# Clustered attention and a gated FFN on one core: another load order and other steps for the preparation of the heads

## The chip, the cores and the metric

The kernel runs on one core of a Trainium2 chip. The metric is device time in microseconds (us), the median of several executions. A profile of one further execution gives the times of single instructions; they are counted from the start of its span. The engines are TensorE (PE, with its weight loads PEld), VectorE (DVE), ScalarE (ACT), GpSimd (POOL) and SyncE (SP, which here only issues transfers). Every engine works through its own list of instructions in the order in which the program wrote them.

## The reference, cut to what matters

```python
batch, n_heads, seq, head_dim = (4, 8, 768, 64);  n_clusters = 16
q_assign = argmax(einsum('bhsd,hcd->bhsc', q_n, c_n), -1)      # k_assign alike
mask = q_assign[..., :, None] == k_assign[..., None, :]
scores = where(mask, matmul(q, k.T) / sqrt(D), -1e9)
attn = softmax(scores);  a = matmul(attn, v)
x = a.transpose(0, 2, 1, 3).reshape(3072, 512)
out = (sigmoid(x @ w_gate) * (x @ w_val)) @ w_out              # 512 -> 1536 -> 512
```

Each query and each key of a head goes to the nearest of 16 centroids, and a query attends only to the keys of its own cluster. The result of all eight heads is the input of a gated feed-forward network.

## The kernel before, in words

**Tiling.** A batch has 8 heads in 4 pairs, 768 positions in 6 chunks of 128. For each head the kernel builds one tile `T` (128 rows, 12 chunks: 6 of keys, 6 of queries). Rows 0 to 63 hold the high half of the fp32 values in fp16; rows 64 to 127 first hold the low half, which the cluster logits need, and then rows 64 to 79 are overwritten with a one-hot row of the cluster: 1 for a key, and -1920 at the wrong clusters for a query. One matmul of a key chunk with the queries then gives score and mask together.

**Steps.** The program is a list of 384 steps, 96 for each batch, which one loop at the end writes out. A step is one scores matmul (`do_scores`, L615: 128 keys by 384 queries, PE L622) and its exponential on ACT (L627). Three steps later in the first batch, and two later in the others, follow the three matmuls with the values (`do_av`, L630, PE L640). In the first batch all heads run first with the first half of the queries (steps 0 to 47, six for each head: head 0 at 0, head 1 at 6, head 4 at 24), then with the second half (48 to 95). From step 57 on, matmuls of the feed-forward network (gate L447, value L467, output L487) are woven in between.

**Preparation of a head.** In the first batch, `first` (L821) makes a head's tile in pieces: `hi` (cast to fp16, L834) and `lo` (the remainder, L841), each once for keys (0) and queries (1); `tu` (six or three 128x128 transposes on PE, L862); `ev` (copy out of PSUM, L873 on ACT, L875 on DVE); `lg` (logits with the centroids, PE L365); `pk` (row maximum L890 and comparison L898, DVE); `ot` (transposes of the one-hot rows, PE L922); and `pl` (copies of these 16 rows into `T`, L943 and L947 on DVE, L945 on ACT). `h2lo1` is piece `lo` of the queries of head 2. `r0` to `r3` are the second halves of the queries of a pair (`rest`, L949). The pieces of the first head are written out by hand (L1057 to L1085 and `lead_in`, L1107). The later batches (`pair_prep`, L1195) use `sp` (split), `tn` (turn of the whole tile by a transposing DMA, L354), `lg`, `pk`, `ot` (one-hot turn by a transposing DMA, L1220) and `hp` (row copies by DMA, `hop`, L428); `b2p0tn0` is the turn of the first head of pair 0 in batch 2. `vc` casts the values (POOL, L282), `vs` sums them (PE L313 in the first batch). `turn_x` (L658) transposes a pair's result for the network.

**What sets the order.** `SCHED`, a table by hand, gives each piece a step. `at` (L672) files the piece under that step, and `run_bg` (L678) writes out all pieces that are due, lowest number first, and pieces of equal number in the order in which they were filed. A number below the current step less a half is raised to it: at the start that is -4.5, so all numbers below -4.5 mean the first slot ahead of step -3. Entries with a final `E` choose the engine of a piece (`A` ACT, `D` DVE, `P` POOL). `nd` entries put small matmuls on constant data into the PE list ahead of a step (`dummies`, L693, does so in the lead-in; `dm` entries give the counts), and `ns` entries say how much of the network is written at each step. A piece whose input is late holds its engine, and all that stands behind it on that engine.

**Loads.** The loop at L1038 issues the first batch's loads on SP: first those of head 0, then `v0, k1, q1, v1, k2, q2, v2, k3, q3, v3` (`k2` is the keys of pair 2, 384 KB; a `q` here is the first half of the queries, 192 KB). The second halves of the queries (`ql`) and the loads of later batches are pieces with steps of their own.

**PSUM.** Scores, logits and value sums share four buffers (`ring`, L147); transposes, one-hot turns and the network's output share two (`op`, L149).

Of the kernel before, what the change touches and what calls it, by code (L numbers as in the profile page):

```python
# [10 lines left out]
AF = mybir.ActivationFunctionType  # L11
ALU = mybir.AluOpType
# [76 lines left out]
def kernel(  # L89
# [164 lines left out]
    def centroid_b():  # L254
        DVE.tensor_scalar(r0, r0, 1e-6, None, ALU.add)
        DVE.reciprocal(r0, r0)
        ACT.activation(c2, cen.unsqueeze(1).to_broadcast([128, 2, D]), AF.Copy, scale=r0)
# [26 lines left out]
    def v_sum(b, p):  # L284
        r, st = RAW["v", b, p], {}

        def one():
            st["a"] = vsp.tile([128, 2, 3, 64], FP, tag="va3", name="va3")
            DVE.tensor_tensor(st["a"], r[:, :, 0:3], r[:, :, 3:6], ALU.add)

        def two():
            a = st["a"]
            s = st["s"] = vss[(b * NP + p) % len(vss)]
            t = vsp.tile([128, 2, 64], FP, tag="va1", name="va1")
            DVE.tensor_tensor(t, a[:, :, 0], a[:, :, 1], ALU.add)
            DVE.tensor_tensor(s[:, :, 0:64], t, a[:, :, 2], ALU.add)
# [375 lines left out]
    def at(i, f):  # L672
        bg.setdefault(max(i, step_no[0] - 0.5), []).append(f)

    def plan(name, step, f):
        at(SCHED.get(name, step), f)
# [518 lines left out]
    def pair_prep(b, p, use):  # L1195
# [26 lines left out]
        def hops(e):  # L1222
            for s in range(2):
                hop(st["ot"], 2 * e + s, T[b, 2 * p + e], 6 * s, 6)
# [105 lines left out]
```

## Time and profile before

| | |
|---|---|
| time, median of 3 runs | 328.78 us (328.36 to 329.84) |
| profiled execution, own time | 330.25 us |
| its span, first to last instruction | 328.4 us |
| PE busy | 321.7 us, 98% |
| ACT busy | 239.5 us, 73% |
| DVE busy | 187.5 us, 57% |
| POOL busy | 107.9 us, 33% |
| read from and written to memory | 28.34 MB and 6.29 MB |

The profiled execution lies 1.47 us above the median, and 1.85 us of it lie outside the span. A row of the timeline has start, length, engine, line, operation, what it writes and reads, shape, count, and in brackets how long the engine stood idle before it and whom it waited for. Matmuls are pipelined: the length of one includes its way through the array, so a row of one matmul of 384 columns shows about 0.33 us although the next can start about 0.16 us after it, and an engine shown as busy may still be held up for a short time. Starts are exact, ends of matmuls are modelled.

### The profile page before, as it was taken

How to read it: one execution, taken by the hardware profiler on the slowest of the kernel's cores; microseconds unless marked ns; L12 is line 12 of the kernel's file. 1: busy time of each engine (PE TensorE's matmuls, PEld its weight loads, DVE VectorE, ACT ScalarE, POOL GpSimd, SP SyncE). 2: the span in 40 equal slices, each digit the busy share in tenths (PEclk: the TensorE clock that was granted, in tenths of full speed). 3: DMA queues.
4: the chain of work that ended last, by engine and by line, in shares of the span. 5: the costliest groups of instructions: out<-in, count | busy, mean ns of one | idle time of the engine just before them, and what ended most of it. 6: DMA issues, size and time to landing. Idle time of an engine off the chain costs nothing.

```text
span 328.4 us, 8945 instructions
## 1 busy us (share of the span) xinstructions
PE 321.7 (98%) x3405; PEld 209.2 (64%) x3405; DVE 187.5 (57%) x531; ACT 239.5 (73%) x547; POOL 107.9 (33%) x149
## 2 busy tenths in 40 slices
PE   8899999999999999999999999999999999999996
PEld 4688866766666666666566655666566665654654
DVE  6688747778658567556556654666534322441431
ACT  6497998887989898877778777788778877332421
POOL 5866464334434375424133343413301111000000
PEclk9799999999999999999999999999999999999999
DMA  6999987728986996975775473752631012102002
GB/s 199 360 247 165 241 164 127 183 62 209 237 173 185 170 213 145 267 151 131 184 216 107 144 134 90 210 121 50 140 92 36 2 26 76 46 1 85 12 0 96
DMA packets 77994, 45.14 MB, mean 137 GB/s; under 512 B 56896, under 2 KB 75008, under 8 KB 77952
## 3 DMA queue, kind: packets, MB, share of 16 engines
q1 hardware_dynamic: 73984, 39.73, 48.6%
q0 software_dynamic: 3680, 4.72, 8.8%
q8 instruction: 26, 0.43, 0.5%
q10 hardware_dynamic: 288, 0.13, 0.1%
q14 instruction: 16, 0.13, 0.1%
HBM read 28.34 MB, written 6.29 MB: 105 GB/s over the span
## 4 chain that ended last, share of the span: by engine, by line
PE 91%; DMA 4%; SPq 2%; ACT 1%; POOL 1%; issue 0%; DVE 0%
PE v L467 18%; PE o L487 18%; PE g L447 18%; PE sc L622 18%; PE av L640 10%; DMA T<-hl 2%; PE lg L378 2%; DMA kraw<-in_k_dram 2%; PE lg L365 1%; PE t_ps L862 1%; ACT es L627 1%; PE o_end L519 1%; PE oh_ps L922 1%; SPq L185 1%; PE sc L619 1%; SPq L429 1%
## 5 line engine op out<-in xcount | busy, mean ns | idle before, releaser
L627 ACT ACTIVATE es<-sc 128x384 f16<-128x384 f32 x384 | 176.2, 494 | 39.2 <-PE sc L622 34.5
L622 PE MATMUL sc<-T 128*128 128x384 f16 x384 | 119.2, 327 | 0.3 <-DVE T L947 0.2
L640 PEld LDWEIGHTS <-es 128*128 128x128 f16 x1152 | 81.8, 98 | 49.3 <-issue 0.2
L640 PE MATMUL av<-va,es 128*128 128x65 f16 x1152 | 97.7, 194 | 0.0
L474 DVE SCALAR_TENSOR_TENSOR hT<-th,v 128x384 f16<-128x384 f32 x96 | 53.1, 553 | 65.7 <-PE av L640 42.5
L467 PE MATMUL v<-xTb,wv 128*128 128x384 f16 x384 | 78.1, 326 | 0.0
L447 PE MATMUL g<-xTb,wg 128*128 128x384 f16 x384 | 78.0, 326 | 0.0
L487 PE MATMUL o<-wo,hT 128*128 128x512 f16 x276 | 75.1, 379 | 0.0
L334 POOL TENSOR_TENSOR xp<-t,rec 128x192 f16<-128x192 f32 (+1 forms) x46 | 29.5, 642 | 129.0 <-DVE rec L331 78.6
L455 ACT ACTIVATE th<-g 128x384 f32<-128x384 f32 x96 | 47.2, 491 | 25.3 <-DVE hT L474 17.9
L447 PEld LDWEIGHTS <-wg 128*128 128x128 f16 x384 | 37.2, 97 | 20.4
L467 PEld LDWEIGHTS <-wv 128*128 128x128 f16 x384 | 37.4, 98 | 20.1 <-issue 0.2
L622 PEld LDWEIGHTS <-T 128*128 128x128 f16 x384 | 37.2, 97 | 0.7 <-DVE T L947 0.4
L487 PEld LDWEIGHTS <-hT 128*128 128x128 f16 x276 | 26.7, 97 | 16.2
L329 DVE TENSOR_TENSOR t<-av,sv 128x195 f32<-128x195 f32 (+1 forms) x46 | 20.1, 437 | 23.8 <-PE av L640 20.6
L1203 POOL TENSOR_TENSOR hl<-kraw,hl 128x384 f16<-128x384 f32 x22 | 20.7, 943 | 25.2 <-DVE hl L1202 13.2
L1203 POOL TENSOR_TENSOR hl<-qraw,hl 128x384 f16<-128x384 f32 x22 | 21.6, 982 | 11.9 <-DVE hl L1202 11.9
L390 DVE TENSOR_TENSOR lgs<-lg,lglo 128x192 f32<-128x192 f32 (+1 forms) x25 | 8.7, 348 | 16.4 <-ACT lglo L384 15.9
L496 ACT ACTIVATE ob<-o 128x512 f32<-128x512 f32 x15 | 8.9, 596 | 10.8 <-PE o L487 10.7
L282 POOL CAST va<-vraw 128x768 f16<-128x768 f32 x16 | 13.4, 840 | 2.1 <-DMA vraw<-in_v_dram 2.1
L494 DVE TENSOR_SCALAR ob<-o 128x512 f32<-128x512 f32 x8 | 5.5, 691 | 13.4 <-PE o L487 13.3
L378 PE MATMUL lg<-cm,T 128*128 128x32 f16 x288 | 11.1, 177 | 0.2 <-DMA T<-hl 0.2
(117 smaller groups left out, 245.3 us busy)
## 6 DMA issues: line engine op xcount, KB each, us to landing
vraw<-in_v_dram SPq DMA_DIRECT2D x16, 384.0 KB, 5.1
out_dram<-ob SPq DMA_DIRECT2D x23, 256.0 KB, 2.3
kraw<-in_k_dram SPq DMA_DIRECT2D x15, 384.0 KB, 4.3
qraw<-in_q_dram SPq DMA_DIRECT2D x12, 384.0 KB, 4.2
wg<-in_moe_w_gate_dram POOLq DMA_DIRECT2D x2, 768.0 KB, 8.6
wv<-in_moe_w_val_dram POOLq DMA_DIRECT2D x2, 768.0 KB, 7.6
wo<-in_moe_w_out_dram POOLq DMA_DIRECT2D x2, 768.0 KB, 8.6
qraw<-in_q_dram SPq DMA_DIRECT2D x7, 192.0 KB, 6.7
```

The costliest lines, as they stand in the source:

```text
L329: DVE.tensor_tensor(t[:, 0:nq, :], av, sv, ALU.add)
L334: (eng or POOL).tensor_tensor(x, t[:, 0:nq, 0:64], bcast(rec[:, 0:nq], 64), ALU.mult)
L378: PE.matmul(out=lg[:, bass.ts(i, 32)], lhsT=t[:, c, :], rhs=cm[:, h].rearrange("p s n -> p (s n)"), start=True, stop=True,)
L447: PE.matmul(out=g[:, 0:n], lhsT=wg[fc // WQ][:, dc, fc % WQ, :], rhs=xT[:, dc, t0 : t0 + n], start=(dc == 0), stop=(dc == NDC - 1),)
L455: ACT.activation(th[:, 0:n], g[:, 0:n], AF.Tanh, scale=0.5)
L467: PE.matmul(out=w[:, 0:n], lhsT=wv[fc // WQ][:, dc, fc % WQ, :], rhs=xT[:, dc, t0 : t0 + n], start=(dc == 0), stop=(dc == NDC - 1),)
L474: DVE.scalar_tensor_tensor(hT[:, fc, 0:n], st[1][:, 0:n], 1.0, w[:, 0:n], ALU.add, ALU.mult)
L487: PE.matmul(out=o, lhsT=hT[:, fc, bass.ts(t, 128)], rhs=wo[fc // WON][:, fc % WON, :], start=(fc == 0), stop=(fc == NFC - 1),)
L622: PE.matmul(out=sc.rearrange("p (c t) -> p c t", t=128), lhsT=s["k"], rhs=s["q"], start=True, stop=True,)
L627: ACT.activation(es, sc, AF.Exp, scale=SCALE)
L640: PE.matmul(out=av[:, s["c0"] + i, :], lhsT=s["es"][:, bass.ts(i, 128)], rhs=VA[b, p][:, e, s["j"], :], start=(first and i == 0), stop=(la ...
L1203: POOL.tensor_tensor(hl[:, :, 64:128], r, hl[:, :, 0:64], ALU.subtract)
```

## The change

241 entries of the table differ. Nearly all move a piece by half a step to four steps; these are the ones that the text below speaks of, one entry to a line:

```diff
+    "lo": ["k1", "v0", "q1", "y0", "v1", "k3", "q2", "q3", "k2", "v2", "v3"],
-    "h1lo1": -3.0, "h1tu1": -0.5, "h1ev0": -0.5, "h1ev1": 0,
+    "h1lo1": -37.5, "h1tu1": -38.5, "h1ev0": -3.5, "h1ev1": -3.5,
-    "h1lo1E": "D",
-    "h1pl0": 2.5, "h1pl1": 1.5,
+    "h1pl0": 1.5, "h1pl1": 3.5, "h1pl1E": "A",
-    "h2hi0": -4.0, "h2hi1": -0.5, "h2hi1E": "P", "h2lo0": -1.5, "h2lo1": 0,
+    "h2hi0": -8.5, "h2hi1": -8.5, "h2hi1E": "A", "h2lo0": -3.5, "h2lo1": -1.5,
-    "vc00": -4.0, "vs00": 1.5,
+    "vc00": -1.0, "vs00": 4.0,
-    "r0hi": 11.0,
+    "r0hi": 6.5,
-    "h3ev1E": "A", "h4pl1E": "A",
+    "h6ev0E": "A",
-    "h4hi0": 1.0, "h4lo0": 5.0, "h4tu0": 10.0, "h4lg": 16.5, "h4pk": 17.0, "h4ot": 20.0,
+    "h4hi0": 2.0, "h4lo0": 4.0, "h4tu0": 9.0, "h4lg": 15.0, "h4pk": 17.5, "h4ot": 21.0,
-    "dm1": 2, "dm4": 3,
+    "dm1": 1, "dm4": 4,
...
+    "b2p0tn0": -47, "b2p0lg0": -35.5, "b2p0lk": 3.5,
-    "b1p1hp0": -19.5, "b1p3ot": -23.5, "b1p3hp1": -12.5,
+    "b1p1hp0": -13.5, "b1p3ot": -19.0, "b1p3hp1": -14.0,
```

Ahead of the change `b2p0tn0` took the value -50 from `b2tn0`, `b2p0lg0` was -37.5, and `b2p0lk` took -0.5 from `b2lk`. `y0` in the new load order issues nothing. In the lists of instructions that the two programs give, PE has 45 in place of 40 of the small matmuls that the `nd` entries add, one of 128 columns less ahead of the first transposes (`dm1`), and one more behind the first scores (`dm4`). All other matmuls, and all transfers, are the same in kind and number; on ACT, DVE and POOL, casts and copies change their engine.

The code gains branches that the table does not switch on; they add no instruction:

```diff
+        cw = cen.unsqueeze(1).to_broadcast([128, 2, D])
+        if SCHED.get("c2d", 0):
+            DVE.tensor_scalar(c2, cw, r0, None, ALU.mult)
...
-    def v_sum(b, p):
+    def v_sum(b, p, eng=None):
...
         def hops(e):
+            if SCHED.get("hop2", 0):
...
-                at(use + o + d_, lambda b=b, p=p, side=side: load(SP, side, b, p))
+                at(use + o + d_, lambda b=b, p=p, side=side: load(
+                    (ACT if SCHED.get("lda", 0) else POOL) if side in SCHED.get("ldp", "") and NP * b + p >= SCHED.get("ldb", 5) else SP, side, b, p))
```

More of the change, by code (lines that the diff above doesn't have):

```diff
@@ L256, in centroid_b @@
         DVE.reciprocal(r0, r0)
-        ACT.activation(c2, cen.unsqueeze(1).to_broadcast([128, 2, D]), AF.Copy, scale=r0)
+        cw = cen.unsqueeze(1).to_broadcast([128, 2, D])
+        if SCHED.get("c2d", 0):
+            DVE.tensor_scalar(c2, cw, r0, None, ALU.mult)
+        else:
+            ACT.activation(c2, cw, AF.Copy, scale=r0)
     def centroid_c():
@@ L282, in v_cast @@
         (cast or POOL.tensor_copy)(va[:, h, :, 0:64], RAW["v", b, p][:, h])
-    def v_sum(b, p):
+    def v_sum(b, p, eng=None):
         r, st = RAW["v", b, p], {}
+        eng = eng or DVE
         def one():
             st["a"] = vsp.tile([128, 2, 3, 64], FP, tag="va3", name="va3")
-            DVE.tensor_tensor(st["a"], r[:, :, 0:3], r[:, :, 3:6], ALU.add)
+            eng.tensor_tensor(st["a"], r[:, :, 0:3], r[:, :, 3:6], ALU.add)
         def two():
@@ L294, in two @@
             t = vsp.tile([128, 2, 64], FP, tag="va1", name="va1")
-            DVE.tensor_tensor(t, a[:, :, 0], a[:, :, 1], ALU.add)
-            DVE.tensor_tensor(s[:, :, 0:64], t, a[:, :, 2], ALU.add)
+            eng.tensor_tensor(t, a[:, :, 0], a[:, :, 1], ALU.add)
+            eng.tensor_tensor(s[:, :, 0:64], t, a[:, :, 2], ALU.add)
         def rest():
@@ L1184 @@
             vf = {}
-            plan(f"vs0{p}", u - 3 if p else 4, lambda p=p, vf=vf: (vf.update(f=v_sum(0, p)), vf["f"][0]()))
-            at(SCHED.get(f"vs0{p}", u) + SCHED.get(f"vt0{p}", 1), lambda vf=vf: (vf["f"][1](), vf["f"][2]()))
+            plan(f"vs0{p}", u - 3 if p else 4, lambda p=p, vf=vf: (vf.update(f=v_sum(0, p, POOL if SCHED.get(f"vq{p}", 0) else DVE)), vf["f"][0]()))
+            at(SCHED.get(f"vs0{p}", u) + SCHED.get(f"vt0{p}", 3), lambda vf=vf: (vf["f"][1](), vf["f"][2]()))
         else:
@@ L1222, in hops @@
         def hops(e):
+            if SCHED.get("hop2", 0):
+                SP.dma_start(
+                    out=T[b, 2 * p + e][64:80].rearrange("x (s c) t -> s x c t", s=2),
+                    in_=st["ot"].rearrange("(y x) c t -> y x c t", x=32)[2 * e : 2 * e + 2, 0:16],
+                )
+                return
             for s in range(2):
```

139 rows, old and new, of the table SCHED are left out of this document.

## The prediction, made before the changed kernel ran

> **What bounds the kernel now.** I read the page's busy times and its chain of waits first, then the table of stretches of 8 us.
>
> ```profile
> PE 321.7 (98%) x3405; PEld 209.2 (64%) x3405; DVE 187.5 (57%) x531; ACT 239.5 (73%) x547; POOL 107.9 (33%) x149
> ...
> PE 91%; DMA 4%; SPq 2%; ACT 1%; POOL 1%; issue 0%; DVE 0%
> ```
>
> ```profile
> 0.00:8.00 8.00, 6.46 (x62) 4.07 (x62) 5.22 (x29) 4.93 (x11) 4.32 (x14) 1.00 0.66 195
> 8.00:16.00 8.00, 6.55 (x94) 5.20 (x92) 5.81 (x18) 3.32 (x8) 6.59 (x11) 0.79 1.08 362
> 16.00:24.00 8.00, 7.77 (x150) 6.58 (x147) 6.22 (x21) 7.92 (x20) 5.42 (x9) 1.00 1.12 255
> 24.00:32.00 8.00, 7.90 (x150) 6.95 (x150) 6.82 (x23) 6.75 (x16) 5.06 (x8) 1.00 0.97 162
> ...
> 104.00:112.00 8.00, 7.79 (x91) 5.14 (x90) 4.50 (x14) 7.30 (x19) 3.67 (x4) 1.00 1.26 237
> ```
>
> The columns of the second are the stretch, its length, busy time of PE, PEld, DVE, ACT and POOL, granted PE clock, DMA share and GB/s. PE carries 91% of the chain. It stands idle 1.54 us in the first 8 us and 1.45 in the next, then 0.23, 0.10, and in the stretch at 104 once more 0.21. Everything else is PE's own list of matmuls, which the change leaves as it is except for a few dummies. So the change can only gain in the first 30 us and at single waits later. In the second stretch PE also had a clock of 0.79, and from 16 to 24 us ACT is as full as PE (7.92 of 8).
>
> The timeline shows where PE loses time at the start:
>
> ```profile
> 7.24 0.34 PE L922 MATMUL oh_ps<-identh,oh 128*128 128x128 f16 x3
> ...
> 7.63 0.83 POOL L282 CAST va<-vraw 128x768 f16<-128x768 f32 x1 [2.11 <-DMA vraw<-in_v_dram]
> ...
> 8.41 0.34 PE L622 MATMUL sc<-T 128*128 128x384 f16 x1 [0.21 <-DVE T L947]
> ...
> 9.20 0.51 ACT L834 CAST hl<-kraw 128x384 f16<-128x384 f32 x1 [1.31 <-DMA kraw<-in_k_dram]
> ...
> 9.61 0.48 ACT L627 ACTIVATE es<-sc 128x384 f16<-128x384 f32 x1
> ...
> 10.00 0.47 ACT L873 COPY T<-t_ps 128x384 f16<-128x384 f16 x1
> ...
> 10.52 0.31 PE L365 MATMUL lg<-cm,T 128*128 128x16 f16 x6 [0.56 <-ACT T L873]
> ...
> 10.75 0.51 PE L862 MATMUL t_ps<-identh,hl 128*128 128x128 f16 x6
> ...
> 11.67 0.34 PE L862 MATMUL t_ps<-identh,hl 128*128 128x128 f16 x3 [0.40 <-POOL hl L841]
> ...
> 11.85 0.48 PE L622 MATMUL sc<-T 128*128 128x384 f16 x1
> ...
> 12.36 0.92 ACT L627 ACTIVATE es<-sc 128x384 f16<-128x384 f32 x2 [1.90 <-PE sc L622]
> ```
>
> The first scores start at 8.41, the second only at 11.85. Between them lies a chain: the keys of pair 1 (`k1`) land at 9.2, ACT stands with their cast at the head of its list, the copy of head 1's queries out of PSUM (`h1ev1`) comes at 10.00, PE's logits wait for it until 10.52, and the last transposes of head 2 wait for POOL until 11.67.
>
> **The change part by part: the start.** Its prices:
>
> ```profile
> 3.59 0.47 SPq L196 DMA_DIRECT2D qraw<-in_q_dram  x1
> ...
> 4.52 0.55 POOL L841 TENSOR_TENSOR hl<-qraw,hl 128x192 f16<-128x192 f32 x1 [0.89 <-ACT hl L834]
> ...
> 6.32 0.34 DVE L834 CAST hl<-qraw 128x192 f16<-128x192 f32 x1
> ...
> 10.64 0.34 POOL L834 CAST hl<-qraw 128x192 f16<-128x192 f32 x1
> ```
>
> ```profile
> DMA to landing us min/median/max: 2.9/6.2/7.3
> ```
>
> The last line is for the query loads of the first 17 us. `k1` takes the place of `v0` and should land at 7.6; `v0` lands at 9.2. `q1` stands behind both as before: 3.59 + 6.2 = 9.8, not ahead of the 9.2 of the load that it follows, and not after 10.64, where its cast began without a wait.
>
> *First scores.* The transposes of head 1's queries (`h1tu1`) now stand ahead of the six logits, five dummies and three one-hot turns at 7.24, and their low part (`h1lo1`) is on POOL. The cast ends at 6.32 + 0.34 = 6.66, the low part at 7.21, 7.27 with a hand-over of 0.06. Then three transposes (a step of 0.055 each, from six in 0.51 against three in 0.34), six logits (0.15) and five dummies (0.28) bring the turns from 7.24 to about 7.9. The first scores come 0.66 later, at 9.07. That alone costs nothing, since the second scores wait for the chain through ACT, which ends after them in either order.
>
> *Second scores.* ACT casts `k1` early, but the cast of `q1` moves from POOL to ACT, ahead of `h1ev1`. ACT waits until 9.8, casts (0.34) and copies (0.47): 10.6, against 10.00 + 0.47 = 10.47 before. PE's logits start 0.13 later, at 10.65, the six transposes at 10.88. The three that waited for POOL do not wait now: their low part starts when ACT's cast ends (10.14) and ends at 10.7. Six steps of 0.055 and the 0.18 from 11.67 to 11.85 give 11.39 in place of 11.85: **-0.45**. With `q1` at 9.2 it would be -1.05, at 10.64 +0.4; I take the median landing and keep both ends.
>
> [...]
>
> **The two loads that come later, or are wanted earlier.**
>
> ```profile
> 9.76 3.06 SPq L196 DMA_DIRECT2D qraw<-in_q_dram  x4
> ...
> 12.71 0.63 POOL L834 CAST hl<-kraw 128x384 f16<-128x384 f32 x1
> ...
> 14.06 0.94 POOL L229 DMA_DIRECT2D wg<-in_moe_w_gate_dram  x1
> ...
> 16.08 0.91 POOL L841 TENSOR_TENSOR hl<-kraw,hl 128x384 f16<-128x384 f32 x1
> ...
> 16.44 1.92 ACT L627 ACTIVATE es<-sc 128x384 f16<-128x384 f32 x4
> ...
> 18.28 0.50 PE L862 MATMUL t_ps<-identh,hl 128*128 128x128 f16 x6
> ```
>
> `k2` goes behind `k3`, `q2` and `q3`, 768 KB or 2.2 us at 362 GB/s. It had landed by 12.71, so it is there by 14.9. POOL then needs the cast (0.63), the issue of the gate weights (0.94), a query cast (0.34) and the low part (0.91): 17.7. Head 4's transposes started at 18.28; with PE 0.45 earlier they are wanted at 17.8. Cost nothing, and up to 0.4 if PE gains more than that. `r0hi` moves on ACT from step 11 to behind the eighth exponential. Its load, first of the four at 9.76, lands by 9.76 + 7.3 = 17.1; the eighth of the exponentials (third of the four at 16.44) ended at about 17.9, less 0.45 is 17.4. Again nothing, and up to 0.6 if ACT is much earlier. `v0` lands 1.6 later, and its cast stands three POOL operations later; the first matmuls with values wait for the first exponential too, now at 10.6.
>
> **Waits that go, and dummies.**
>
> ```profile
> 15.75 0.79 ACT L873 COPY T<-t_ps 128x768 f16<-128x768 f16 x1
> ...
> 23.48 0.26 PE L640 MATMUL av<-va,es 128*128 128x65 f16 x3
> ...
> 23.97 0.49 PE L922 MATMUL oh_ps<-identh,oh 128*128 128x128 f16 x6 [0.23 <-DVE T L875]
> ...
> 25.71 0.48 ACT L945 ACTIVATE T<-oh_ps 16x384 f16<-16x384 f16 x1
> ```
>
> ```profile
> 110.81 0.32 PE L622 MATMUL sc<-T 128*128 128x384 f16 x1
> ...
> 111.35 0.47 PE L378 MATMUL lg<-cm,T 128*128 128x32 f16 x12 [0.21 <-DMA T<-hl]
> ```
>
> The one-hot turns of head 4 could follow the value matmuls 0.09 after 23.48, but start 0.40 later, when DVE has emptied their PSUM buffer of head 5's transposes. The change puts head 4's logits 1.5 steps and that copy (`h5ev0`) 0.5 earlier, and the turns one step later: **-0.40**, at worst 0. The copy of head 4's query rows (0.48) leaves ACT for DVE, just ahead of head 4's scores: I take half, **-0.25**, between 0 and -0.48. In its place ACT gets a copy of 768 columns for head 6 (0.79), which the 1.25 us that ACT is idle from 24 to 32 should hide.
>
> At 111.35 the logits of batch 2's first head wait for its turn. The scores ahead take 0.16, so 0.38 is lost. The logits go two steps later and the turn three; if it lands when it did, behind loads that were issued ahead of it, the wait goes, and if it lands later with its issue, it grows by a step (0.6). I take **-0.20**, between -0.38 and +0.6. The other moves in later batches lie under a full PE: nothing to gain, and two new waits like this one, 0.8, is what I allow for. Five more dummies cost 5 x 0.055: **+0.28**; the one less (`dm1`) stands where PE waits.
>
> **Sum.** -0.45 - 0.40 - 0.25 - 0.20 + 0.28 = -1.02. Against the profiled execution's own 330.25 us (span 328.4 and 1.85 around it) that is 329.2. The median of the runs shown is 328.78, 1.47 less; I carry the same difference over: **327.8 us**.
>
> **The rivals.**
>
> *The clock stays up: 326.5 us.* The 0.79 from 8 to 16 us:
>
> ```profile
> 12.55 0.85 PE L922 MATMUL oh_ps<-identh,oh 128*128 128x128 f16 x6
> ...
> 16.22 0.50 PE L922 MATMUL oh_ps<-identh,oh 128*128 128x128 f16 x6
> ```
>
> Six turns take 0.85 behind the long gap and 0.50 later. At half clock, 0.21 x 8 / 0.5 = 3.4 us of the stretch, or 1.7 us of lost work; I price it at 1.4, since PE waits in part of it. If two scores ahead of 11.85 are work enough, that goes, less a little for `k2`: -1.3 on the forecast. For it: more matmuls in the gap; against it: the gap from 9.07 to 11.4 is still mostly waiting. [...]
>
> *What is gained is waited for again: 328.8 us.* POOL is busy 6.59 of 8 us and stands behind `k2`, ACT behind `q1` and `r0hi`. If these are later than I take them, PE's 0.45 is used up at head 4's transposes, and the two waits of 0.65 at heads 4 and 5 come back at heads 5 and 6; the dummies and batch 2 cancel.
>
> *ACT becomes the bound: 330.7 us, slower.* The first exponential moves from 9.61 to about 10.6 (+1.0), behind the cast of `q1`. ACT gains a cast (0.34), the row copy `h1pl1` (0.48) and the copy for head 6 (0.79), and loses copies of 0.47 and 0.48: +0.66. From 16 to 24 ACT is already full. If the exponentials set the pace to the end of the first batch's lead, this and the dummies add 1.9. It decides if ACT's waits of 1.90 ahead of 12.36 and after it do not shrink by 1.6 together; I think that they shrink by about that, since the second scores come earlier.
>
> **How the numbers follow.** Forecast 0.45 (its own range 327.1 to 328.5), clock 0.22, waited for again 0.21, ACT 0.12. Low end: the clock's case with the wider start, 326.0. High end 330.0, short of the ACT case: with it and the tails below 326.0, no more than 2 in 10 are left out. Half a per cent, about what a measurement of this kernel can tell from no change, is 1.64 us: below 327.14 is faster, above 330.42 slower. Faster: the clock's 0.22 and 0.08 of the forecast, 0.30. Slower: 0.12. Within: 0.58.
>
> **What the new profile would show.** Right: ACT's second cast of the lead waits for `qraw` until about 9.8; first scores at 9.1, second at 11.4; no wait of PE for DVE ahead of head 4's turns; no wait for `T<-hl` at 111. Wrong: second scores at 11.85 or later (the start gave nothing); PE waiting for POOL ahead of head 4's transposes; ACT waiting for `qraw` at its cast of 384 columns near 17 us; a clock of 1.00 from 8 to 16 (then the second case); or ACT busy over 7.9 from 24 to 32 with PE below 7.8 (the last).

## The result, and the profile after

The changed kernel is slower. Its median is 330.68 us over 16 executions, against 328.47 us over 17 before: ratio **1.0059, 95% interval 1.0043 to 1.0075**, some 1.9 us. A 17th execution of the changed kernel took 666 us and is left out everywhere. A second comparison gave 330.68 against 328.73, ratio 1.0061 (1.0044 to 1.0077). The forecast was 327.8 with a range up to 330.0.

The profiled executions alone mislead. That of the changed kernel had a span of 327.6 us, shorter than the 328.4 of the kernel before. But the 16 executions of the changed kernel have spans from 327.1 to 330.8, median 328.45: its profile shows one of the shorter ones. Of the 107 executions of the kernel before that were run beside the experiments, 98 had a granted clock of 0.998 or more and a median span of 327.0; nine had 0.995 and 327.9 to 329.4, median 328.5. The profile on which the prediction rests was of that kind (0.995, 328.4). So the kernel before was profiled in one of its longer executions and the changed one in one of its shorter. I therefore compare with a further profile of the kernel before, at its usual clock, called `before_again` below (span 326.5). By the medians of the spans the loss is 1.45 us; the rest lies outside the span, where the changed kernel's executions have 1.8 to 3.6 us and those 107 have 1.7 to 2.1. No profile shows that part.

The page of the changed kernel, busy times and chain:

```profile
PE 321.0 (98%) x3410; PEld 208.9 (64%) x3410; DVE 187.4 (57%) x528; ACT 239.6 (73%) x547; POOL 109.0 (33%) x152
...
PE 91%; DMA 6%; SPq 1%; issue 0%; POOL 0%; ACT 0%; DVE 0%; POOLq 0%
```

DMA has 6% of the chain, 4% before. Two tables of stretches follow, first the changed kernel, then `before_again` (stretch, length, busy time of PE, PEld, DVE, ACT, POOL, PE clock, DMA share, GB/s):

```profile
8.00:16.00 8.00, 7.35 (x137) 6.33 (x135) 6.66 (x19) 5.66 (x13) 7.34 (x11) 1.00 1.08 360
16.00:24.00 8.00, 7.42 (x147) 6.18 (x144) 7.53 (x22) 6.88 (x18) 7.46 (x15) 1.00 1.14 263
24.00:32.00 8.00, 8.00 (x167) 7.06 (x164) 7.49 (x25) 7.21 (x16) 3.94 (x7) 1.00 1.07 184
104.00:112.00 8.00, 8.00 (x93) 5.33 (x92) 4.54 (x12) 7.41 (x19) 4.45 (x6) 1.00 1.01 161
200.00:208.00 8.00, 7.42 (x79) 4.56 (x77) 3.26 (x11) 5.86 (x14) 2.80 (x4) 1.00 0.64 173
```

```profile
8.00:16.00 8.00, 6.94 (x122) 5.66 (x121) 7.02 (x21) 5.08 (x11) 7.11 (x12) 1.00 1.07 357
16.00:24.00 8.00, 7.76 (x159) 6.58 (x156) 6.65 (x23) 7.85 (x20) 5.96 (x12) 1.00 1.14 262
24.00:32.00 8.00, 7.90 (x157) 6.94 (x155) 6.64 (x22) 6.40 (x15) 5.01 (x7) 1.00 1.08 188
104.00:112.00 8.00, 7.83 (x94) 5.19 (x91) 4.30 (x13) 7.09 (x18) 3.27 (x4) 1.00 1.17 211
200.00:208.00 8.00, 8.00 (x86) 5.01 (x83) 3.68 (x12) 6.55 (x17) 3.32 (x5) 1.00 0.53 141
```

PE is fuller from 8 to 16, from 24 to 32 and at 104, where the prediction had its gains. It is emptier in two stretches where the prediction's sum had no cost: from 16 to 24 us (7.42 against 7.76), and from 200 to 208 (7.42 against 8.00).

What PE waited for names both places, and a third before them; the table of PE's waits of the changed kernel (line, what released it, sum, times, longest), then that of `before_again`:

```profile
...
PE g L461 <- DMA xTb<-xp: 0.6, 1, 0.6
PE sc L636 <- DVE sv L333: 0.5, 1, 0.5
PE oh_ps L936 <- DVE T L889: 0.4, 1, 0.4
...
```

```profile
...
PE t_ps L862 <- POOL hl L841: 0.5, 1, 0.5
PE oh_ps L922 <- DVE T L875: 0.5, 2, 0.3
PE sc L622 <- DVE T L947: 0.2, 1, 0.2
PE lg L378 <- DMA T<-hl: 0.2, 1, 0.2
...
```

(L636, L461, L936 and L889 of the changed code are L622, L447, L922 and L875 of the code before.) The third is the first row of the changed kernel's timeline that follows: the one-hot turns of head 1 stand at 11.55 until DVE has copied transposes of head 2 out of the PSUM buffers that both use. At the same turns (11.72) `before_again` loses 0.20, here 0.61 are lost. The other rows are around 17 us:

```profile
11.55 0.49 PE L936 MATMUL oh_ps<-identh,oh 128*128 128x128 f16 x6 [0.44 <-DVE T L889]
...
15.16 0.92 POOL L855 TENSOR_TENSOR hl<-kraw,hl 128x384 f16<-128x384 f32 x1
15.37 1.70 DVE L855 TENSOR_TENSOR hl<-qraw,hl 128x192 f16<-128x192 f32 x1
...
16.03 0.82 POOL L295 CAST va<-vraw 128x768 f16<-128x768 f32 x1
...
16.67 0.26 PE L654 MATMUL av<-va,es 128*128 128x65 f16 x3
...
16.88 0.51 ACT L972 CAST hl<-qraw 128x384 f16<-128x384 f32 x1 [1.06 <-DMA qraw<-in_q_dram]
17.10 0.29 DVE L333 TENSOR_SCALAR sv<-vs_ps 128x130 f32<-128x130 f32 x1
...
17.45 0.32 PE L636 MATMUL sc<-T 128*128 128x384 f16 x1 [0.52 <-DVE sv L333]
```

and of `before_again` at the same work:

```profile
15.39 0.91 POOL L841 TENSOR_TENSOR hl<-kraw,hl 128x384 f16<-128x384 f32 x1
...
15.90 0.29 DVE L319 TENSOR_SCALAR sv<-vs_ps 128x130 f32<-128x130 f32 x1
16.11 0.42 DVE L841 TENSOR_TENSOR hl<-qraw,hl 128x192 f16<-128x192 f32 x1
```

Scores and value sums share four PSUM buffers. `sv` (piece `vs01`) copies a value sum out and so frees one. The change files the low part of head 4's queries (`h4lo1`, step 7.5 to 6.5) ahead of it (`vs01`, step 7.0 to 6.5). That low part took 0.42 us before; here it takes 1.70, beside two POOL operations. PE's scores, which could follow at 16.8, start at 17.45. The DVE operation ended at 17.07, 0.22 after POOL's cast of the values (16.03 + 0.82 = 16.85). In all eight traces in which this operation took so long, it ended 0.22 to 0.23 after POOL's second operation. What ties the two together no run shows.

The second place in the changed kernel:

```profile
200.53 1.20 SPq L681 DMA_TRANSPOSE xTb<-xp  x1
...
203.19 0.65 PE L461 MATMUL g<-xTb,wg 128*128 128x384 f16 x3
...
204.42 0.32 PE L461 MATMUL g<-xTb,wg 128*128 128x384 f16 x1 [0.58 <-DMA xTb<-xp]
```

The transposition `xTb` of the third batch's last pair landed 3.85 us after its issue (204.38). In `before_again` it took 2.37 us (issue 200.06), and PE did not wait.

### The profile page after: what moved, and what is told of

Read it like the earlier page. It is cut to its first block, busy times and chain, and to the rows that moved or that the text cites. A ratio compares the mean times of both kernels' runs of the same rounds, so it can differ in the third digit from the quotient of the medians.

```text
span 327.6 us, 8946 instructions
## 1 busy us (share of the span) xinstructions
PE 321.0 (98%) x3410; PEld 208.9 (64%) x3410; DVE 187.4 (57%) x528; ACT 239.6 (73%) x547; POOL 109.0 (33%) x152
## 4 chain that ended last, share of the span: by engine, by line
PE 91%; DMA 6%; SPq 1%; issue 0%; POOL 0%; ACT 0%; DVE 0%; POOLq 0%
PE v L481 19%; PE g L461 19%; PE sc L636 18%; PE o L501 17%; PE av L654 10%; DMA qraw<-in_q_dram 4%; PE lg L392 2%; DMA xTb<-xp 1%; PE lg L379 1%; PE o_end L533 1%; PE sc L633 1%; DMA T<-ohT 1%; PE oh_ps L936 1%; PE t_ps L876 1%; PE t_ps L759 0%
## 5 line engine op out<-in xcount | busy, mean ns | idle before, releaser
L641 ACT ACTIVATE es<-sc 128x384 f16<-128x384 f32 x384 | 175.7, 493 | 37.5 <-PE sc L636 30.8
L636 PE MATMUL sc<-T 128*128 128x384 f16 x384 | 118.4, 325 | 0.8 <-DVE sv L333 0.5
L461 PE MATMUL g<-xTb,wg 128*128 128x384 f16 x384 | 78.2, 326 | 0.6 <-DMA xTb<-xp 0.6
L461 PEld LDWEIGHTS <-wg 128*128 128x128 f16 x384 | 37.1, 97 | 20.4 <-issue 0.2
L636 PEld LDWEIGHTS <-T 128*128 128x128 f16 x384 | 37.1, 97 | 0.2 <-DVE T L961 0.2
```

Source lines behind the costliest of these rows:

```text
L461: PE.matmul(out=g[:, 0:n], lhsT=wg[fc // WQ][:, dc, fc % WQ, :], rhs=xT[:, dc, t0 : t0 + n], start=(dc == 0), stop=(dc == NDC - 1),)
L636: PE.matmul(out=sc.rearrange("p (c t) -> p c t", t=128), lhsT=s["k"], rhs=s["q"], start=True, stop=True,)
L641: ACT.activation(es, sc, AF.Exp, scale=SCALE)
```

## The experiments

All kernels are the changed kernel's code with entries of the table set to the old or the new values. Medians are compared with the kernel before on the same chip.

**Do the parts add up?** `before_again` and `after_again` repeat the two kernels. `first_only` has the new values of the first batch alone (135 entries), `later_only` those of the later batches alone (106).

> The kernel before once more, to see in how many executions TensorE falls to half clock near 12 us, as it did in the profiled one (clock 0.79 from 8 to 16 us). Theory A (in most executions of the kernel before the clock stays up, and the profiled one was an exception): span about 326.7 us in most executions, clock 1.0, and no half-clock stretch in this profile. Theory B (the stretch is always there): span 328.4, clock 0.995.

> The changed kernel once more: 330.7 us, ratio 1.006. Theory A (waits on transfers that land a little later from run to run): spans between 327 and 331, and in this profile other waits, or longer ones, than in the first: ACT for the second half of pair 0's queries near 17 us (1.06 us in the first), matmuls of the network for a transposed result near 203 us (0.74 us in the first). Theory B (the waits are the same in each execution): spans within 0.5 us of 327.6 and the same waits.

> Only the entries for the first batch (load order, its pieces, dummies, casts and sums of values, turns of results) are the changed ones; the second and later batches have the steps of before. Theory S (the loss is in the start): ratio 1.006, as the whole change. Theory L (the loss is in the later batches' moves): ratio below 1.000, between 0.997 and 1.000.

> Only the entries for the second and later batches are the changed ones; the first batch is as before. Theory L (the loss is in the later batches' moves): ratio 1.004 to 1.008, with waits of TensorE for transposes or row copies after 60 us that the kernel before does not have. Theory S (the loss is in the start): ratio 0.998 to 1.001.

```
before_again  328.79 (ratio 1.0004)    after_again  330.68 (1.0061)
first_only    329.16 (1.0008)          later_only   328.60 (1.0004)
```

Neither half costs anything that the ratios show (1.0008, 0.9996 to 1.0021, and 1.0004, 0.9990 to 1.0017); together they cost 0.6%. Both theories that put the loss into one half fall. `after_again`'s trace had the hold near 203.5 us again (landing after 3.84 us); neither half's trace had it (2.38 and 2.30).

**Undoing single parts, and adding halves of the later entries.**

```diff
 after_r0hi11   (changed kernel)            after_no_nd86  (changed kernel)
-    "r0hi": 6.5,                           -    "nd86": 2, "nd87": 1,
+    "r0hi": 11.0,
 first_plus_b1: first_only + entries g, b1, nd86, nd87
 first_plus_b2: first_only + entries b2, xs10, vso
```

> The changed kernel with one entry put back: r0hi at step 11 in place of 6.5. Theory E (the early cast costs PE its waits near 17 us): ACT no longer waits 1.06 us for qraw near 17 us, PE's holds of 0.68 and 0.22 near 17 us go, and the median is 329.8 (330.68 less 0.9). Theory M (most of the loss is a matter of moments, a transfer in the third batch that is slow when it meets another one): all later times come 0.9 earlier, the hold of 0.74 near 203.5 may go as well, and the median is 329.0. Rival W (the gain is waited for again at the next late piece): holds near 17 us go, others of the same size come by 35 us, median 330.5 or above.

> The changed kernel without the three small matmuls ahead of steps 86 and 87. Plain sum: 3 x 0.055 = 0.17 us less, median 330.5, and the hold of 0.74 near 203.5 stays (theory F, a wait that the order of the pieces fixes). Theory M: moments shift by 0.17 us and the number of PE instructions by 3; the transposition xTb near 200 us then takes 2.4 us as in the other kernels, or another transfer is slow; the median moves by over 0.4 us in either direction.

> The changes of the first batch together with those of the second batch's heads (entries g, b1, nd86 and nd87), those of the third and fourth batch, of xs10 and of the value sums as before. Theory F: either this kernel or the one with the third and fourth batch's changes has the whole loss: 330.6 here and 329.2 there, or the other way round. Theory M: both lie between, 329.2 to 330.2, with a wider spread between executions than before (over 1 us from the lowest to the highest).

> The changes of the first batch together with those of the third and fourth batch (entries b2, xs10 and the buffers of the value sums), those of the second batch as before. Theory F: 330.6 or 329.2, the opposite of the kernel with the second batch's changes; if 330.6, the hold of 0.74 near 203.5 is in its trace. Theory M: 329.2 to 330.2 with a wide spread between executions.

Measured: 330.09 (1.0042, 1.0028 to 1.0056), **329.58** (1.0032, 1.002 to 1.0044), 330.83 (1.0065) and 330.01 (1.0039). Three small matmuls, 0.17 us of work, are worth 0.9 us by the ratios (1.1 by the medians), with an uncertainty of some 0.7 us. The hold near 204 us is in the traces of `after_r0hi11` (landing after 4.11 us) and `first_plus_b1` (4.13), not in those of `after_no_nd86` and `first_plus_b2` (2.30 each). Only kernels with nd86 and nd87 *and* the new start had it, at different moments (it began at 203.7 to 204.1). So a fixed wait of one half's pieces does not explain it. In `after_r0hi11` the hold at 17 us was gone, but PE stood 0.57 us ahead of 25.41 for a low part of head 6 on POOL: part of what was gained was waited for again.

**Is it PE's number of instructions?** The records of transfers show a queue of its own for instructions: 26 packets of 16 KB in the span, some 13 us apart in the second half. PE has 3410 matmuls and as many weight loads; 6820 / 26 is 262 for each packet. From this count alone I take them for PE's instructions; no run shows what a block holds. The transfers of the changed kernel between issue and landing of the transposition (200.53 to 204.38), then those of `before_again` (200.06 to 202.44), then those of `after_no_nd86` (200.86 to 203.16):

```profile
q8 instruction: 1, 0.02, 1.6%
...
xTb<-xp SPq DMA_TRANSPOSE x1, 3.8
```

```profile
q1 hardware_dynamic: 416, 0.10, 20.4%
...
xTb<-xp SPq DMA_TRANSPOSE x1, 2.4
```

```profile
q1 hardware_dynamic: 416, 0.10, 21.2%
q14 instruction: 1, 0.01, 1.3%
...
xTb<-xp SPq DMA_TRANSPOSE x1, 2.3
```

Columns are packets, MB and share of time; queue 8 carries the 16 KB blocks. One falls into the transposition only in the first. Theory I: small matmuls ahead move the block against the transposition, which then lands late and holds PE up; it is a guess from these traces. Four kernels:

```diff
 nd_moved       (changed kernel)            before_nd200   (kernel before)
-    "nd86": 2, "nd87": 1,                  +    "nd200": 6,
+    "nd200": 3,
 start_only: kernel before + the new entries of the start (loads, heads 1 and 2, r0hi, nd2 to nd15)
 mid_later:  kernel before + all other new entries except nd86 and nd87
```

> The changed kernel with the three small matmuls taken from ahead of steps 86 and 87 and put ahead of step 200 (near 136 us). [...]

> The kernel before with six small matmuls more ahead of step 200, and nothing else. Plain sum: 6 x 0.055 = 0.33 us, median 329.0. Theory I: twelve PE instructions more ahead of 200 us bring the load of the block of instructions from 2.49 us behind the issue of xTb to 1.8 us or less; xTb then lands after 3.8 us or more, PE is held up by 0.7 us or more near 203 us, median 329.8. If the block comes before xTb is issued, or behind its landing as now, the plain sum holds and the theory isn't shown by this run.

> Only the entries of the start: order of loads, heads 1 and 2, r0hi, first casts of the values, and the dummies of the first 15 steps (three more). Reading of the traces: PE's idle time up to 12 us is as before within 0.3 us, ACT waits about 1.0 us for qraw near 17 us and PE is held 0.9 there, the hold of 0.40 ahead of head 4's turns stays: median 329.7 to 330.0. My prediction's steps would have it at -0.45 + 0.17, median 328.4.

> The start as before, all else as in the changed kernel, but without the three small matmuls ahead of 86 and 87. Reading of the traces: the holds of 0.40 and 0.27 at heads 4 and 5 and of 0.33 at 109 us go, new ones of 0.2 at 66 and 0.2 at 93 us come: median 328.1 to 328.4, faster than both kernels by a little. Theory I: another 0.5 to 1.0 more if a load of a block of instructions falls into a transposition that PE waits for. Rival (what is gained is waited for again): holds of the same size come between 16 and 40 us, median 328.7 or above.

Measured: `nd_moved` 330.74 (1.0059, 1.0046 to 1.0072), the time that theory I has, since the three still stand ahead of the transposition: that of the changed kernel (330.68), not of the one without them (329.58); `before_nd200` **330.83** (1.0055, 1.0034 to 1.0076), where the plain sum is 329.0 and theory I had 329.8; `start_only` 330.62 (1.0061), above both expectations; `mid_later` **328.25** (0.9982, 0.9969 to 0.9994), faster than both kernels. The trace of `before_nd200` has the hold in a kernel that is unchanged but for six matmuls ahead of step 200, first the timeline, then the transfers from 202.03 to 206.37:

```profile
204.68 0.65 PE L809 MATMUL g<-xTb,wg 128*128 128x384 f16 x3
206.37 0.58 SPq L542 DMA_DIRECT2D qraw<-in_q_dram  x1
206.41 0.32 PE L809 MATMUL g<-xTb,wg 128*128 128x384 f16 x1 [1.08 <-DMA xTb<-xp]
```

```profile
q8 instruction: 1, 0.02, 2.2%
...
xTb<-xp SPq DMA_TRANSPOSE x1, 4.3
```

`start_only` had it as well (landing after 4.24). The profiled execution of `nd_moved` had no hold: it is the short one of its five (span 327.2, the others 328.7 to 329.4). I take the other four to have had it, but that is not shown: of no kernel are there two traces, one with the hold and one without. `before_nd200` falls apart in the same way (three spans of 327.8 to 328.5, three of 329.6, though two of the long ones, the profiled one among them, had a clock of 0.993 and 0.994). Its four executions at the usual clock have a median span of 328.3, some 1.1 us above the kernel before on that chip, so that part of the 1.8 us is the clock of the other two.

**Is it the wait, and is it the place?** `before_nd300` puts the six matmuls behind the transposition. The cover kernels let the network's matmuls run a little later, so that the first one that needs `xTb` stands two steps later.

```diff
 before_nd300   (kernel before)             before_nd200_cover  (kernel before)
+    "nd300": 6,                            +    "nd200": 10,
 after_cover (changed kernel), mid_later_cover (mid_later), before_nd200_cover:
-    "ns22": 500, "ns23": 510,
+    "ns22": 460, "ns23": 480,
```

> The kernel before with six small matmuls more ahead of step 300, behind the transposition near 200 us. Theory I: no instruction ahead of that transposition has changed, it lands as before, only the plain sum of 6 x 0.055 = 0.33 us is left: median 329.1. Rival (six more matmuls cost 1.9 us wherever they stand): 330.7.

> The kernel before with ten small matmuls more ahead of step 200, and with the network's matmuls written out a little more slowly in pairs 2 and 3 of the third batch (ns22 460, ns23 480), so that the first of them that needs xTb stands two steps later, about 1.7 us, with others of the network's ahead of it. Ten, since some eight instructions of the network now stand behind the transposition. Theory I: xTb still lands 3.8 us or more after its issue in the trace, or does not, but PE is not held up for it: plain sum 10 x 0.055 = 0.55 us, median 329.3. Rival (what costs is not the wait): 330.8 or more.

> The changed kernel with the same two entries (ns22 460, ns23 480). Theory I: no hold near 203.5; the median falls by the 0.74 us of that hold or somewhat more, to 329.7 to 330.0, and the spread between executions becomes narrower. Rival: 330.7 as before the entries.

> The kernel with the start of before and the later entries of the change (without the three matmuls at 86 and 87), with ns22 460 and ns23 480. Its trace had no such hold. Theory I: the same median, 328.2, at most with fewer executions above 329. If most of its executions had the wait, 327.6.

Measured: 329.98 (1.0030, 1.0013 to 1.0048), 330.94 (1.0064), 329.94 (1.0043, 1.0026 to 1.0060) and 329.01 (1.0004).

`after_cover` has the time that theory I has, 0.7 us lower by the medians and 0.5 by the ratios, though the intervals overlap. It doesn't show that the cover helped: in its trace `xTb` landed after 2.31 us, with no block beside it. `before_nd200_cover` split theory I in two. Its `xTb` landed 4.84 us after issue, the latest of all, and PE, two steps later, did not wait; but the median did not fall. Two new waits for the network's order took 0.4 and 0.2 us (they are in the traces of all three cover kernels, most of `mid_later_cover`'s +0.7), and another block of 16 KB came at 323.5 us, beside the last stores. Their landing in this kernel, then in `before_again` (the issues from 322 us on; a row of two gives their median):

```profile
out_dram<-ob_end SPq DMA_DIRECT2D x1, 128.0 KB, 3.4
out_dram<-ob_end SPq DMA_DIRECT2D x2, 64.0 KB, 2.4
```

```profile
out_dram<-ob_end SPq DMA_DIRECT2D x1, 128.0 KB, 1.7
out_dram<-ob_end SPq DMA_DIRECT2D x2, 64.0 KB, 1.5
```

The first two of these three stores landed 1.7 and 1.5 us later after their issue, the last was issued 0.8 us later behind the first, and from the start of PE's last matmul to the end of the span went 4.35 us in place of 3.38. (In all other 19 traces that is 3.37 to 3.41, and no block lies beside the stores.)

`before_nd300` is a miss: 0.9 above theory I. Its spans lie in two groups (five of 326.8 to 327.4, seven of 327.9 to 329.2). Three of the upper group had a clock of 0.995 to 0.997; the nine others have a median span of 327.4, 0.4 above the kernel before, which is near the plain sum (0.33), so the miss may in part be these three. The profile shows one of the upper group at full clock. Its step 48 starts 0.77 us later than in `before_again`, and it has another late turn, at a place that the six matmuls do not precede:

```profile
138.95 0.41 PE L740 MATMUL lg<-cm,T 128*128 128x32 f16 x10 [0.62 <-DMA T<-hl]
```

SP had needed 2.64 us to issue a transposition at 126.75 (1.19 in `before_again`, at 126.06), and this turn behind it landed at 138.91, in `before_again` at 137.22. No block of 16 KB lies beside the turn, and beside the transposition lies one in both traces (127.50 and 127.02). So a block of instructions is not the only thing that makes a transposition late, and why this kernel is slow so often stays open.

All 20 traces for `xTb` near 200 us, in us after its issue (start of the nearest 16 KB block behind the issue, landing):

```
late:    after 1.77, 3.85    after_again 1.74, 3.84    after_r0hi11 1.82, 4.11    first_plus_b1 1.79, 4.13
         start_only 1.80, 4.24    before_nd200 1.96, 4.34    before_nd200_cover 2.28, 4.84
in time: nd_moved 2.12, 2.31    mid_later 2.39, 2.31    lead_mid_later 2.44, 2.30    before_again 2.48, 2.37
         first_only 2.49, 2.38    later_only 2.49, 2.30    before 2.56, 2.38    the other six: no block up to 3.3, 2.30 to 2.37
```

All seven late ones had a block that began while the transposition was under way. Of the thirteen others only one had, 0.19 us before the landing. That the two go together is shown, and that a few small matmuls ahead can bring it about.

The packets show what is late. In all 20 traces the 384 packets of 256 bytes that carry the transposition's data have ended 1.83 us after its issue. Then come packets of 4 bytes: in the thirteen 32 of them, the last by 2.02 us, and the landing 0.29 to 0.37 after that; in each of the seven late ones 30. The row for the first 2.17 us of the changed kernel's transposition (200.53 to 202.70) has two packets fewer than the 416 that the thirteen have by then:

```profile
q1 hardware_dynamic: 414, 0.10, 22.4%
```

In six of the seven the two missing ones come within 0.02 us of the end of the block, here at 203.29 and 203.30, and the landing follows 0.84 to 1.21 after it. So the data are not late; two closing packets are, and they come when the block is through. That the block holds them up is the plain reading, but it remains argued: in the seventh (`before_nd200_cover`) the block's record begins at 2.28, after the two were due, and other small packets hide when they came; and the longer time from these packets to the landing is not explained.

**What does the start cost?** With `mid_later` (neither) and `after_no_nd86` (both), two more kernels make a table of two by two: `lead_mid_later` adds the new start with `r0hi` at 11, `r0hi_mid_later` adds `r0hi` at 6.5 alone.

> mid_later with the changed start, but r0hi at step 11 as before. If the prediction's step for the second scores (-0.45) is right and carries on: median 327.8 to 328.0. Reading of the traces so far: the second scores come 0.4 earlier, but head 6's transposes near 24.5 us wait 0.7 for POOL, step 48 starts near 37.2 in place of 36.6, median 328.6 to 329.2.

> mid_later with r0hi at step 6.5, all else of the start as before. If the early cast alone costs what the holds near 17 us show (0.68 and 0.22): median 328.9 to 329.2, step 48 near 37.4. If the cost comes only with the new order of the loads: 328.3, step 48 near 36.7. In both, the transposition xTb near 200 us can land late by its own chance; it is read from the trace.

```
neither   mid_later       328.25  ratio 0.9982 (0.9969 to 0.9994)   step 48 starts at 36.79
r0hi      r0hi_mid_later  328.83        0.9992 (0.9972 to 1.0011)                     38.29
start     lead_mid_later  329.41        1.0008 (0.9993 to 1.0023)                     37.57
both      after_no_nd86   329.58        1.0032 (1.0020 to 1.0044)                     37.49
```

(The profile of `r0hi_mid_later` had the clock of 0.995, so its step 48 doesn't compare.) By the ratios the start costs 0.9 us (three more small matmuls, 0.17, among it), `r0hi` 0.3 alone and 0.8 beside the start, each with an uncertainty of 0.6 to 0.8 us, and the kernels ran on three chips. The cost of `r0hi` beside the start is not seen in the traces of the two kernels: step 48 starts at 37.57 without and 37.49 with it. My reading that `r0hi` brings the hold at 17 us falls: with `r0hi` at 11, `lead_mid_later` has it in full. Rows of DVE and PE in its timeline:

```profile
15.92 1.70 DVE L1242 TENSOR_TENSOR hl<-qraw,hl 128x192 f16<-128x192 f32 x1
17.65 0.29 DVE L720 TENSOR_SCALAR sv<-vs_ps 128x130 f32<-128x130 f32 x1
...
18.00 0.32 PE L1023 MATMUL sc<-T 128*128 128x384 f16 x1 [0.52 <-DVE sv L720]
```

In the eight traces with `h4lo1` of 1.66 to 1.73 us ahead of `sv`, PE is held 0.64 to 0.70 at this point. In `after_r0hi11` the same operation, in the same order, took 0.94, and there was no hold. There it ended 0.22 after POOL's first operation, and POOL's cast of the values took 0.97 in place of 0.82. So the order of the two on DVE does not bring the hold by itself; what else it takes no run shows. In `mid_later` it took 0.61, with a hold of 0.12. Putting `vs01` ahead of `h4lo1` again by itself was not tried.

## Why the prediction was wrong, point by point

- **Second scores, -0.45.** The mechanism was right. They start 1.5 to 1.8 us after `q1` lands in ten of the eleven traces with the new start, and 2.1 to 2.3 us after it in the nine with the old one, 10.62 against 11.14 in the two profiles compared above. `q1` itself lands anywhere from 8.75 to 10.01 in either order; 11.85, from which I counted, was near the late end.
- **The step that failed first, and most: the -0.45 carried to the end, with "cost nothing" for `k2`, "again nothing" for `r0hi`, and DVE not looked at.** I followed the pieces that move on ACT and POOL, and priced `k2` and `r0hi` by whether their data would be there. From the second scores to step 12 (scores at 18.54, in `before_again` at 17.80) PE has one small matmul more and otherwise the same ones, but takes 7.92 us in place of 6.66. The holds that make the difference are the one at 11.55 (0.61 for 0.20), where the one-hot turns wait for DVE's copies; the one at 17.45 (0.65), where the exchange of `h4lo1` and `vs01` on DVE leaves PE's score buffer occupied; and 0.23 at 17.83, where an exponential stands behind the cast of `r0hi`, whose data kept ACT waiting for 1.06. So the gain is more than used up. This is the case "what is gained is waited for again", at another engine than I named. By the ratios the start and `r0hi` together cost 1.6 us where the forecast had them at -0.45.
- **Head 4's turns, -0.40; row copy, -0.25; logits of batch 2, -0.20.** Right. The waits are gone from the traces (0.40, 0.27 and 0.33 in `before_again`; a new one of 0.17 stands near 34 us), and `mid_later`, which has these gains without the new start, is 0.18% faster, 0.6 us. Rows of the changed kernel, with no wait in brackets:

```profile
22.81 0.44 PE L936 MATMUL oh_ps<-identh,oh 128*128 128x128 f16 x5
...
110.97 0.45 PE L392 MATMUL lg<-cm,T 128*128 128x32 f16 x12
```

- **Dummies, +0.28.** Right as work: PE has 3410 matmuls in place of 3405. Wrong as cost: three of the five are worth 0.9 us. With them goes the late landing of `xTb`; that they bring it about through where PE's instructions are loaded is argued.
- **The second step that failed: "the other moves in later batches lie under a full PE: nothing to gain", with 0.8 allowed for two new waits.** There are two new waits of 0.2 us each (67 and 93 us), and a hold of 0.74 us near 204 in both traces of the changed kernel (0.74 to 1.25 in the six traces that have it). PE had 3.15 us of other work between the issue of `xTb` (200.53) and the matmul that needs it (it could have started at 203.68), so that a landing after 2.3 us left 0.8 to spare. I had not searched for places where so little is to spare.
- **The reference.** Gains were read from an execution with the clock of 0.995, whose 1.47 us above the median I carried over whole. In its trace the clock was 0.50 from 12 to 15 us, 0.94 in the microsecond ahead of that and 0.85 in the one behind it; in that of `before_again`, the same code, it was 1.00 from 8 to 16. The rival "the clock stays up" was wrong for the median: 98 of 107 executions before had a clock of 0.998 or more, so there was nothing for it to gain. That two scores in the gap would keep the clock up was my estimate; no run shows it.
- **ACT becomes the bound** did not happen: ACT is busy 6.88 of 8 us from 16 to 24, less than before. Its 330.7 us is the measured time by luck, since the loss came by another mechanism.

Along the chain before, `mid_later`, `lead_mid_later`, `after_no_nd86`, changed kernel the ratios give the loss of 1.9 us as -0.6 for the middle and later entries, +0.9 for the start, +0.8 for `r0hi` and +0.9 for the matmuls at 86 and 87 with the hold that goes with them. Each of the last three is uncertain by 0.6 to 0.8 us.

## What to carry to other kernels

For each transfer that PE waits for or nearly waits for, read how much other work lies between its issue and its use: 0.8 us to spare at one place can be a loss at the next change, wherever that is. Follow a move on every engine, and look for what frees the buffer that the bound engine takes next, not only for what brings its data. Before reading gains from one profile, see where that execution lies among the others by span and clock.

## What the runs showed of the hardware that was not expected

- A block of 16 KB, which I take for PE's instructions, is loaded 26 or 27 times in a trace. Where one began 1.7 to 2.3 us after the issue of a transposition that otherwise lands after 2.3 us, the landing came after 3.8 to 4.8 us in seven of eight traces. The data had been moved as early as ever; in six of the seven, two of the 32 closing packets of 4 bytes came only at the end of the block. Beside the last stores, two of these landed 1.7 and 1.5 us later.
- Six matmuls of 0.055 us ahead of it made a kernel 1.8 us slower (1.0055), some 1.1 us if executions at the usual clock alone are compared.
- A DVE operation on 192 columns with two inputs took 0.35 us at its shortest, and up to 1.73 beside two POOL operations; it ended 0.22 to 0.23 after the second.
- Nine of 107 executions of the same program had a granted clock of 0.995 and were 1.5 us longer.
- `q1`, one of the first loads, lands at 8.75 to 10.01 us in the 20 traces, and at 9.75 and 8.87 in the two of the same kernel before.
